# Scales by DMA, layer 1's weights split during layer 0, and layer 1's high part on ScalarE a unit late

## The chip, the cores and the metric

The kernel runs on one core of a Trainium2 chip. The metric is the device time in microseconds (us) of one execution, the median of several runs; less is better. The core's engines, each with its own queue of instructions that it works through in order, are TensorE (PE: matmuls; PEld: their weight loads), VectorE (DVE), ScalarE (ACT), GpSimd (POOL) and SyncE (SP, which here issues every DMA). TensorE has two clocks, 1.2 and 2.4 GHz; a "granted clock" of 1.00 is the higher one.

## The reference

All in float32. `x` is (2, 4096, 192), so 8192 tokens of 192 numbers.

```
conv:     out[s, h, :] = sum over k of softmax(weight[h])[k] * x[s - 6 + k, h, :]     (8 heads, 7 taps, causal)
layer 0:  h = conv @ w_in;   g = h * sigmoid(h);                        y = g @ w_out  (192 -> 2048 -> 192)
layer 1:  h = y @ w_in2;     g = h if h > 0 else exp(min(h, 0)) - 1;    out = g @ w_out2
```

The inputs arrive as float64 or float32 words laid out by the host; weights come as 64-bit words.

## The kernel before, in words

Tokens are cut into 16 blocks of 512 (`NB`), the 2048 inner columns into 8 pieces of 256 (`NQ`). A **unit** (layer, block, piece) is the work of one piece for one block: *in-products* (18 matmuls, `in_products`) make `h`, 256 x 512, in one of two PSUM buffers; `act_steps` makes `g` from it and splits `g` into a high part `g_hi`, in the type that TensorE multiplies, and a low part, the rest; *out-products* add the piece's share to four PSUM sums. Numbers are kept precise by such splits: a product is high x high plus high x low plus low x high. Layer 0 has 128 units, then layer 1 has 128. Blocks 0 and 1 of layer 0 go together in pairs at the start; block 2 uses full out-products of 20 matmuls. From block 3 of layer 0 on, and in all of layer 1, blocks are **scaled**: `g` is multiplied by a power of two `forth`, the low part is kept in float16 in a ring of 12 buffers, and a unit's out-products are only 12 matmuls (`high_products`); the low parts of a block's eight units are multiplied together at the end of the block (`low_products`, 32 + 64 short matmuls, lines 603 and 615). The sums are then scaled back, stored in memory after layer 0 and fetched again for layer 1.

The scale of a block needs the largest magnitudes over all 128 partitions: `measure` reduces on VectorE, GpSimd's `partition_all_reduce` (line 382) adds over the partitions, and `set_scale` makes `forth` and `back` with six tiny VectorE instructions (lines 411 to 419). The weights have such a scale too (`up`, `down`). Layer 0's output weights are brought to theirs by `rescale(q)` in units 19 to 26: ScalarE rounds them to float16 (line 215), VectorE makes the rest (lines 217, 221), ScalarE writes the rounded part back (line 225).

Order is written by hand. The main loop (line 1045) takes unit `s`: its in-products, the table `fill[s]` of side work, its `act_steps`, and the out-products of unit `s - LAG`, two units earlier. `at(step, f)` puts side work into the table; `where` is a unit's number. Side work is: the convolution taps on VectorE for the next block, splitting it (`split_conv`), fetching and splitting layer 1's input (`load_mid`, `split_mid`), and layer 1's weights. These are loaded once in blocks 5 to 8 to find their largest value (`measure_raw`), and again near the end of layer 0: from block 14 on `next_w` decodes piece q (64-bit words to float32: one ScalarE and three VectorE instructions, lines 138 to 149) and `split_w` splits it into `wi` and `wo` (ScalarE, GpSimd line 160, VectorE line 177), all inside the last units of layer 0 and the first of layer 1.

In layer 1 a unit's `act_steps` are, in this order:

```
ScalarE  g = relu(-h)            line 530        VectorE  g_hi = g * forth           line 535
ScalarE  g = exp(-g)             line 531        VectorE  lo = g * forth - g_hi      line 538
VectorE  g = max(g - 1, h)       line 532        (h's PSUM buffer is free after line 532)
```

In layer 0 they are silu in place (ScalarE, line 525), `g_hi` (ScalarE, line 526) and `lo` (VectorE, line 538, after which `h`'s buffer is free). As `h` has two buffers, the in-products of unit u + 2 wait until unit u has freed its own.

Of the kernel before, what the change touches and what calls it, by code (L numbers as in the profile page):

```python
# [40 lines left out]
RING = 12  # L41
# [5 lines left out]
def kernel(  # L47
# [114 lines left out]
    def split_w(layer, q, cols, eng, copy=None):  # L162
# [8 lines left out]
        if layer == 1:  # L171
            val = val[:, OUT].rearrange("p (i d) -> p i d", d=D)
            w16 = new_w16(layer, q)
            nc.scalar.activation(out=w16, in_=val, func=ACTF.Copy, scale=up[1])
            nc.scalar.activation(out=wo[:, :, 0:D], in_=w16, func=ACTF.Copy)
            for src, to in LOWS:
                nc.vector.scalar_tensor_tensor(
                    out=wo[:, :, to], in0=val[:, :, src], scalar=up[1], in1=wo[:, :, src].bitcast(F32),
                    op0=ALU.mult, op1=ALU.subtract,
                )  # L180
            return
# [9 lines left out]
    LOWS = (slice(P, D), slice(D, D + HP)), (slice(0, P), slice(D + HP, 2 * D))  # L191

# [18 lines left out]
    def rescale(q):  # L211
# [13 lines left out]
        nc.scalar.activation(out=wo[:, :, 0:D], in_=w16, func=ACTF.Copy)  # L225
# [182 lines left out]
    def set_scale(layer, b):  # L408
        t = stat[layer, b]
        total = small(tag="total")  # L410
        nc.vector.tensor_add(out=total, in0=t[:, 0:1], in1=t[:, 1:2])
# [9 lines left out]
    def set_weight_scale(layer, of):  # L421

        m = most[layer] = fixed.tile([P, 2], F32, tag=f"most{layer}", name="most")
# [6 lines left out]
        all_reduce(m, REDUCE.max)  # L430

    def finish_weight_scale(layer):
        largest = small(tag="total")
# [75 lines left out]

    def act_steps(u):  # L510

        h = h_t.pop(u)
        hi = gp.tile([P, 2, TB], F32R, tag="g_hi", name="g_hi")
        if scaled(*u[:2]):
# [4 lines left out]
        g = h if u[0] == 0 and u not in in_tmp else tmp.tile([P, 2, TB], F32, tag="g", name="g")  # L519
        g_of[u] = g  # L520
        if scaled(*u[:2]):
            s = forth[u[:2]]
            if u[0] == 0:
                steps = [
                    lambda: nc.scalar.activation(out=g, in_=h, func=ACTF.Silu),  # L525
                    lambda: nc.scalar.activation(out=hi, in_=g, func=ACTF.Copy, scale=s),  # L526
                ]
            else:
                steps = [
                    lambda: nc.scalar.activation(out=g, in_=h, func=ACTF.Relu, scale=-1.0),  # L530
                    lambda: nc.scalar.activation(out=g, in_=g, func=ACTF.Exp, scale=-1.0),  # L531
                    lambda: nc.vector.scalar_tensor_tensor(  # L532
                        out=g, in0=g, scalar=-1.0, in1=h, op0=ALU.add, op1=ALU.max
                    ),
                    lambda: nc.vector.tensor_scalar_mul(hi, g, s),  # L535
                ]
            return steps + [
                lambda: nc.vector.scalar_tensor_tensor(  # L538
                    out=lo, in0=g, scalar=s, in1=hi.bitcast(F32), op0=ALU.mult, op1=ALU.subtract
                )  # L540
            ]
        if u[0] == 0:
            steps = [
                lambda: nc.scalar.activation(out=hi, in_=h, func=ACTF.Silu),
                lambda: nc.scalar.activation(out=g, in_=h, func=ACTF.Silu),
            ]
        return steps + [lambda: nc.vector.tensor_sub(out=lo, in0=g, in1=hi.bitcast(F32))]
# [201 lines left out]
    LAG = 2  # L749
# [35 lines left out]
    for b in range(2, NB):  # L785
# [4 lines left out]
        if b >= NEW:  # L790
            steps += [lambda b=b: measure(0, b, conv_t[b, 0], conv_t[b, 1])]
            at(s - 1, lambda b=b: set_scale(0, b))
# [8 lines left out]
    at(TWO, lambda: set_weight_scale(0, found))  # L801
    at(TWO + LAG, lambda: finish_weight_scale(0))
    for q in range(NQ):
        at(TWO + LAG + 1 + q, lambda q=q: rescale(q))
        at(where[0, 5, 0] + 3 * q, lambda q=q: load_w(1, q))
        at(where[0, 5, 0] + 3 * q + 3, lambda q=q: measure_raw(q))
    at(where[0, 5, 0] + 3 * NQ, lambda: set_weight_scale(1, found))
    at(where[0, 5, 0] + 3 * NQ + 2, lambda: finish_weight_scale(1))

    def val_of_w2(q):
        if q in (3, 4):
            t = tmp.tile([P, 2, TB], F32, tag="g", name="val_g")
# [317 lines left out]
```

## Time and profile before

| | |
|---|---|
| median of 3 runs | 1134.26 us (1131.65 to 1134.41) |
| the profiled execution | 1132.55 us, of which the span is 1130.5 us, 2.05 us lie around it |
| TensorE matmul busy | 1087.0 us, 96% of the span |
| VectorE, ScalarE, GpSimd busy | 914.4 (81%), 679.6 (60%), 56.4 us (5%) |
| mean granted clock | 0.992 |
| DMA queue of SyncE | 66.06 MB, 21.7% of the 16 engines |

A busy share is a mean over stages with different limits; what a stage can win is read from the spacing of its matmuls. Every scaled block ends with the same low products, so the time from one block's to the next's is the time of a block.

### The profile page before, as it was taken

The numbers are of one execution on the slowest core, as the hardware profiler recorded it, in microseconds if no ns is written. First come the engines' busy times: TensorE is split into PE (matmuls) and PEld (weight loads), VectorE is DVE, ScalarE is ACT, GpSimd is POOL, SyncE is SP. The second block draws the span as 40 slices with busy tenths as digits, with TensorE's granted clock in tenths as the row PEclk, the third lists the DMA queues.
The fourth block names the chain that finished last, engine by engine and source line by source line (L and its number), as shares of the span: only waits on it lengthen the run. The fifth ranks groups of instructions, "written<-read, shape, count | busy, mean of one in ns | idle before, by whom it ended". The sixth has DMA issues, their size and how long they took to land.

```text
span 1130.5 us, 25043 instructions
## 1 busy us (share of the span) xinstructions
PE 1087.0 (96%) x10755; PEld 837.3 (74%) x10755; DVE 914.4 (81%) x1257; ACT 679.6 (60%) x773; POOL 56.4 (5%) x82
## 2 busy tenths in 40 slices
PE   7999889999999999989999999999999999999998
PEld 5998577777787777767767777777777776777776
DVE  6998676677777667668788988888988889888888
ACT  5764556655666666567875565555565565655654
POOL 4430000000000000000110000000000000000000
PEclk8999989999999999999999999999999999999999
DMA  4421023323322221254311111101111101111000
GB/s 126 149 51 49 23 56 86 82 88 100 99 57 57 57 57 30 54 143 124 102 35 33 38 52 53 52 18 50 38 52 52 50 18 39 52 52 52 25 25 15
DMA packets 41087, 67.65 MB, mean 60 GB/s; under 512 B 5392, under 2 KB 17936, under 8 KB 40976
## 3 DMA queue, kind: packets, MB, share of 16 engines
q1 hardware_dynamic: 40976, 66.06, 21.7%
q8 instruction: 84, 1.38, 0.5%
q14 instruction: 27, 0.22, 0.1%
HBM read 33.66 MB, written 12.58 MB: 41 GB/s over the span
## 4 chain that ended last, share of the span: by engine, by line
PE 57%; DVE 25%; issue 8%; ACT 7%; DMA 1%; SPq 1%; DVEq 0%; POOL 0%; ACTq 0%
PE h L503 27%; DVE g L532 10%; PE ab L591 9%; PE ab L615 9%; DVE g_hi L535 5%; PE c L603 5%; PE c L591 5%; DVE lo L538 3%; PE ab L664 2%; DVE x_hl L160 2%; ACT g L531 2%; DVE sum L387 2%; ACT g L530 2%; PE c L664 1%; DVE conv L458 1%
## 5 line engine op out<-in xcount | busy, mean ns | idle before, releaser
L503 PE MATMUL h<-x_hl,wi 64*128 64x512 f32 x4464 | 581.5, 392 | 32.9 <-DVE g L532 15.1
L503 PEld LDWEIGHTS h<-x_hl,wi 64*128 64x128 f32 x4464 | 433.0, 185 | 143.3 <-DVE g L532 28.8
L591 PE MATMUL ab<-g_hi,wo 64*128 64x512 f32 x1856 | 250.1, 387 | 0.0
L530 ACT ACTIVATE g<-h 128x1024 f32<-128x1024 f32 x128 | 131.6, 1028 | 163.1 <-PE h L503 160.5
L591 PEld LDWEIGHTS ab<-g_hi,wo 64*128 64x128 f32 x1856 | 175.8, 184 | 36.7 <-DVE mid_ab L710 0.4
L538 DVE SCALAR_TENSOR_TENSOR lo<-h,forth,g_hi 128x1024 f16<-128x1024 f32 x104 | 133.2, 1281 | 78.9 <-ACT g_hi L526 78.7
L532 DVE SCALAR_TENSOR_TENSOR g<-g,h 128x1024 f32<-128x1024 f32 x128 | 155.5, 1215 | 39.4 <-ACT g L531 36.4
L538 DVE SCALAR_TENSOR_TENSOR lo<-g,forth,g_hi 128x1024 f16<-128x1024 f32 x128 | 164.4, 1284 | 4.5
L525 ACT ACTIVATE h<-h 128x1024 f32<-128x1024 f32 x104 | 104.9, 1009 | 94.5 <-PE h L503 94.5
L591 PE MATMUL c<-g_hi,wo 64*128 64x512 f32 x928 | 144.4, 387 | 0.0
L531 ACT ACTIVATE g<-g 128x1024 f32<-128x1024 f32 x128 | 135.8, 1061 | 4.0
L526 ACT ACTIVATE g_hi<-h,forth 128x1024 fp32r<-128x1024 f32 x104 | 116.2, 1117 | 3.4
L458 DVE SCALAR_TENSOR_TENSOR conv<-x_raw,tap_w,conv 128x512 f32<-128x512 f32 (+1 forms) x174 | 103.8, 635 | 0.2
L591 PEld LDWEIGHTS c<-g_hi,wo 64*128 64x128 f32 x928 | 88.0, 185 | 18.5 <-issue 0.4
L615 PE MATMUL ab<-lo,w 64*64 64x512 f16 x1792 | 101.5, 376 | 0.0
L535 DVE TENSOR_SCALAR g_hi<-g,forth 128x1024 fp32r<-128x1024 f32 x128 | 97.0, 758 | 4.7
L615 PEld LDWEIGHTS <-w 64*64 64x64 f16 x1920 | 55.9, 107 | 44.4
L382 POOL PARTITION_ALL_REDUCE sum<-sum x29 | 11.9, 410 | 905.4 <-DVE sum L387 905.4
L603 PE MATMUL c<-lo,w 64*64 64x512 f16 x928 | 55.9, 379 | 0.0
L603 PEld LDWEIGHTS <-w 64*64 64x64 f16 x928 | 24.5, 106 | 27.7 <-issue 10.6
L715 ACT ACTIVATE o<-ab,back 128x512 f32<-128x512 f32 x16 | 11.0, 690 | 46.7 <-PE ab L615 41.5
L715 ACT ACTIVATE both<-c,back 128x512 f32<-128x512 f32 x29 | 19.9, 688 | 30.2 <-PE c L603 30.2
(135 smaller groups left out, 792.9 us busy)
## 6 DMA issues: line engine op xcount, KB each, us to landing
x_hl<-x_hl SPq DMA_DIRECT2D x60, 256.0 KB, 3.7
raw<-in_w_dram SPq DMA_DIRECT2D x21, 512.0 KB, 4.6
raw<-in_w_dram SPq DMA_DIRECT2D x51, 128.0 KB, 3.6
x_raw<-in_xT_dram SPq DMA_DIRECT2D x16, 259.0 KB, 4.0
kept_ab<-mid_ab SPq DMA_DIRECT2D x16, 256.0 KB, 2.0
mid_ab<-kept_ab SPq DMA_DIRECT2D x16, 256.0 KB, 4.0
mid_c<-kept_c SPq DMA_DIRECT2D x32, 128.0 KB, 3.8
x_hl<-x_hl SPq DMA_DIRECT2D x30, 128.0 KB, 3.8
```

What stands on the lines that cost most here:

```text
L458: nc.vector.scalar_tensor_tensor(out=y, in0=x, scalar=w, in1=y, op0=ALU.mult, op1=ALU.add)
L503: nc.tensor.matmul(out=h[:, r, :], lhsT=w[ROWS[r], w_lo, ts(of, P)], rhs=x_part(layer, b, 3 * x_lo + part)[ROWS[r], :], start=n == 0, stop ...
L525: lambda: nc.scalar.activation(out=g, in_=h, func=ACTF.Silu),
L526: lambda: nc.scalar.activation(out=hi, in_=g, func=ACTF.Copy, scale=s),
L530: lambda: nc.scalar.activation(out=g, in_=h, func=ACTF.Relu, scale=-1.0),
L531: lambda: nc.scalar.activation(out=g, in_=g, func=ACTF.Exp, scale=-1.0),
L532: lambda: nc.vector.scalar_tensor_tensor(out=g, in0=g, scalar=-1.0, in1=h, op0=ALU.add, op1=ALU.max),
L535: lambda: nc.vector.tensor_scalar_mul(hi, g, s),
L538: lambda: nc.vector.scalar_tensor_tensor(out=lo, in0=g, scalar=s, in1=hi.bitcast(F32), op0=ALU.mult, op1=ALU.subtract)
L591: nc.tensor.matmul(out=acc_t[layer, b, f"{name}{r}"], lhsT=wo[ROWS[r], i, ts(k, P)], rhs=hi[ROWS[r], i, :], start=q == 0 and n in (0, 2), ...
L603: nc.tensor.matmul(out=acc_t[layer, b, f"c{r}"][ROWS[i], :], lhsT=w16_t[layer, q][ROWS[r], i, P:D], rhs=g_t[u][1][ROWS[r], i, :], start=Fa ...
L615: nc.tensor.matmul(out=bank[ROWS[j], :], lhsT=w16_t[layer, q][ROWS[r], i, ts(j, HP)], rhs=g_t[u][1][ROWS[r], i, tokens], start=first and i ...
```

## The change

- **Scales.** `all_reduce` goes. `share` writes the 128 x 2 numbers to memory, `fetch` reads them back as 256 numbers on every partition, and a VectorE reduction over 256 columns takes the place of the first tiny instruction of `set_scale`. `fetch` is put two steps ahead of `set_scale`, `set_scale(1, b)` and `split_mid` one step earlier than before.
- **Layer 1's weights.** Piece by piece, one every five units from block 9 on, `made_steps` decodes and splits them in layer 0 (pieces 1 to 7, then 0) into one spare buffer and stores them in memory; in block 15 and the first units of layer 1 `bring` fetches them into the buffers that layer 0's pieces leave. Piece 0 stays where it was made. `rescale`'s last instruction becomes `rescale_end`, a unit later.
- **Layer 1's `act_steps`.** The high part becomes a ScalarE instruction, and it and the low part are held back until the next unit's `g` is made. `g` lies in the buffers of the raw weights.
- **Out-products** come three units late instead of two from unit 27 on (`turn` is 26, a step without any); one is made up for three units before the end. The ring has 11 buffers, `g_hi` uses six.

```
+    def made_steps(q):
...
+        return [
+            lambda: (mag(), low()),
+            lambda: (high(), last()),
+            lambda: copy(wi[:, 0, :], val[:, IN]),
+            lambda: lower(wi[:, 1, :], val[:, IN], wi[:, 0, :]),
+            lambda: nc.scalar.activation(out=w16, in_=v, func=ACTF.Copy, scale=up[1]),
+            lambda: copy(wo[:, :, 0:D], w16),
+            lambda: scale_low(*LOWS[0]),
+            lambda: scale_low(*LOWS[1]),
+            send,
+        ]
...
-    def all_reduce(t, op):
-        nc.gpsimd.partition_all_reduce(t, t, P, op)
+    def share(key, t):
+
+        shared[key] = tc.dram_tile([1, 2 * P], F32, name="shared")
+        nc.sync.dma_start(out=shared[key].rearrange("a (p n) -> (a p) n", n=2), in_=t)
+
+    def fetch(key):
+        t = fixed.tile([P, 2 * P], F32, tag="all", name="all")
+        nc.sync.dma_start(out=t, in_=shared[key].to_broadcast([P, 2 * P]))
+        shared[key] = t
...
-        nc.vector.tensor_add(out=total, in0=t[:, 0:1], in1=t[:, 1:2])
+        nc.vector.tensor_reduce(out=total, in_=shared[layer, b], axis=AX.X, op=ALU.add)
...
+        before = [held.pop(0) for _ in range(len(held))]
+        if u in units[-2:]:
+            before.append(lambda: nc.vector.tensor_scalar_mul(hi, g, s))
+            before.append(low)
+        else:
+            held.extend((high, low))
+        return steps + before
...
-        at(where[1, b, 0] - 5, lambda b=b: split_mid(b))
-        at(where[1, b, 0] - 1, lambda b=b: set_scale(1, b))
+        at(where[1, b, 0] - 6, lambda b=b: split_mid(b))
+        at(where[1, b, 0] - 4, lambda b=b: fetch((1, b)))
+        at(where[1, b, 0] - 2, lambda b=b: set_scale(1, b))
...
+        at(TWO + LAG + 2 + q, lambda q=q: rescale_end(q))
...
+    for k, q in enumerate([*range(1, NQ), 0]):
+        s = look + 8 + 5 * k
+        at(s - 7, lambda q=q: load_w(1, q))
+        at(s, lambda q=q: made.update({q: made_steps(q)}))
+        for i in range(9):
+            at(s + i // 2, lambda q=q, i=i: made[q][i]())
...
+        for k in range(2):
+            at(base + q + k * LATE, lambda q=q, k=k: bring(q, k))
```

How the order moves, at three places. **ScalarE in the middle of a block of layer 1**, two units before the change (L530 relu, L531 exp):

```order
L530 ACTIVATE g<-h 128x1024
L531 ACTIVATE g<-g 128x1024
L530 ACTIVATE g<-h 128x1024
L531 ACTIVATE g<-g 128x1024
L715 ACTIVATE both<-c_10428,back 128x512
```

and after it (L591 relu, L592 exp, L581 the high part):

```order
L591 ACTIVATE g<-h 128x1024
L592 ACTIVATE g<-g 128x1024
L581 ACTIVATE g_hi<-g,forth 128x1024
L591 ACTIVATE g<-h 128x1024
L592 ACTIVATE g<-g 128x1024
L581 ACTIVATE g_hi<-g,forth 128x1024
L771 ACTIVATE both<-c_11940,back 128x512
```

A third full-width instruction stands between two units; it belongs to the unit before.

**VectorE around the end of a block in layer 0**, from the sums (`both`, `mid_ab`) to the next unit's low part (`lo`), before:

```order
L706 SCALAR_TENSOR_TENSOR mid_ab<-ab_4511,back,mid_ab 128x512
L458 SCALAR_TENSOR_TENSOR conv<-x_raw,tap_w,conv 128x512
L458 SCALAR_TENSOR_TENSOR conv<-x_raw,tap_w,conv 128x256
L742 TENSOR_TENSOR other<-both,other 64x512
L458 SCALAR_TENSOR_TENSOR conv<-x_raw,tap_w,conv 128x512
L458 SCALAR_TENSOR_TENSOR conv<-x_raw,tap_w,conv 128x256
L458 SCALAR_TENSOR_TENSOR conv<-x_raw,tap_w,conv 128x512
L538 SCALAR_TENSOR_TENSOR lo_4942<-h,forth,g_hi 128x1024
```

and after, in block 10, where a piece of layer 1's weights is decoded (`val`) and split (`wi`) there:

```order
L762 SCALAR_TENSOR_TENSOR mid_ab<-ab_4599,back,mid_ab 128x512
L502 SCALAR_TENSOR_TENSOR conv<-x_raw,tap_w,conv 128x512
L502 SCALAR_TENSOR_TENSOR conv<-x_raw,tap_w,conv 128x256
L502 SCALAR_TENSOR_TENSOR conv<-x_raw,tap_w,conv 128x512
L140 TENSOR_SCALAR val<-raw 128x768
L144 TENSOR_SCALAR val<-raw 128x768
L148 SCALAR_TENSOR_TENSOR val<-mag,val 128x768
L798 TENSOR_TENSOR other<-both,other 64x512
L502 SCALAR_TENSOR_TENSOR conv<-x_raw,tap_w,conv 128x256
L428 TENSOR_REDUCE sum<-conv 128x1 x2
L367 TENSOR_TENSOR wi<-val,wi 128x384
L584 SCALAR_TENSOR_TENSOR lo_5070<-h,forth,g_hi 128x1024
```

Four instructions of the weights stand between the sums and `lo`, and the two reductions `sum` have moved ahead of this `lo`.

**ScalarE during the rescaling**, units 21 and 22 (`w_...` is the float16 part, `wo` the weights it goes back to, `g_hi` and `h` the two silus of block 2), before:

```order
L215 ACTIVATE w_1429<-wo,up 128x384
L225 ACTIVATE wo<-w_1429 128x2x192
L544 ACTIVATE g_hi<-h 128x1024
L545 ACTIVATE h<-h 128x1024
L215 ACTIVATE w_1480<-wo,up 128x384
L225 ACTIVATE wo<-w_1480 128x2x192
```

and after:

```order
L245 ACTIVATE w_1435<-wo,up 128x384
L574 ACTIVATE g_hi<-h 128x1024
L575 ACTIVATE h<-h 128x1024
L257 ACTIVATE wo<-w_1435 128x2x192
L245 ACTIVATE w_1488<-wo,up 128x384
```

The write back of `wo`, which needs VectorE's reading of the same weights, now stands behind the unit's two silus.

## Rows read from the trace of the kernel before

**Rows 1.** Windows: stretch; length; busy PE, PEld, DVE, ACT, POOL; PE clock; DMA share; GB/s.

```profile
400.00:450.00 50.00, 50.00 (x539) 37.47 (x536) 33.26 (x52) 30.16 (x34) 0.80 (x2) 1.00 0.19 49
700.00:750.00 50.00, 48.80 (x496) 36.59 (x496) 45.89 (x56) 28.62 (x31) 0.40 (x1) 1.00 0.11 30
```

**Rows 2.** Timeline (start, duration, instruction): first low products of blocks.

```profile
435.95 1.92 PE L603 MATMUL c<-lo,w 64*64 64x512 f16 x32
468.68 1.92 PE L603 MATMUL c<-lo,w 64*64 64x512 f16 x32
506.92 1.92 PE L603 MATMUL c<-lo,w 64*64 64x512 f16 x32
539.75 1.92 PE L603 MATMUL c<-lo,w 64*64 64x512 f16 x32
575.93 1.92 PE L603 MATMUL c<-lo,w 64*64 64x512 f16 x32
1091.79 1.92 PE L603 MATMUL c<-lo,w 64*64 64x512 f16 x32
```

**Rows 3.** Waits, 610 to 1120 us: waiter, releaser, total us, times, longest.

```profile
PE h L503 <- DVE g L532: 14.3, 24, 0.9
```

**Rows 4.** Groups by line and form: count, busy us, mean ns, idle before and releaser.

```profile
L535 DVE TENSOR_SCALAR g_hi<-g,forth 128x1024 fp32r<-128x1024 f32 x128 | 97.0, 758 | 4.7
L526 ACT ACTIVATE g_hi<-h,forth 128x1024 fp32r<-128x1024 f32 x104 | 116.2, 1117 | 3.4
L530 ACT ACTIVATE g<-h 128x1024 f32<-128x1024 f32 x128 | 131.6, 1028 | 163.1 <-PE h L503 160.5 <-DVE g L532 2.6
L531 ACT ACTIVATE g<-g 128x1024 f32<-128x1024 f32 x128 | 135.8, 1061 | 4.0
L532 DVE SCALAR_TENSOR_TENSOR g<-g,h 128x1024 f32<-128x1024 f32 x128 | 155.5, 1215 | 39.4 <-ACT g L531 36.4 <-issue 2.7
```

**Rows 5.** Timeline of layer 0: in-products of two units, a low part between.

```profile
444.78 2.20 PE L503 MATMUL h<-x_hl,wi 64*128 64x512 f32 x18
446.14 1.27 DVE L538 SCALAR_TENSOR_TENSOR lo<-h,forth,g_hi 128x1024 f16<-128x1024 f32 x1
448.18 2.20 PE L503 MATMUL h<-x_hl,wi 64*128 64x512 f32 x18
```

**Rows 6.** Timeline: late weights in layer 0, on ScalarE.

```profile
493.89 0.91 ACT L138 ACTIVATE mag<-raw 128x768 f32<-128x768 f32 x1 [5.18 <-DMA raw<-in_w_dram]
```

**Rows 7.** Timeline: decoding and splitting one piece of layer 1's weights.

```profile
547.16 0.59 DVE L141 TENSOR_SCALAR val_x<-raw 128x768 uint16<-128x768 uint16 x1
548.35 0.96 DVE L149 SCALAR_TENSOR_TENSOR val_x<-mag,val_x 128x768 int32<-128x768 int32 x1
553.16 0.74 DVE L177 SCALAR_TENSOR_TENSOR wo<-val,up,wo 128x128 fp32r<-128x128 f32 x2
```

**Rows 8.** Timeline: in-products of units 20 and 28, around the rescaling.

```profile
105.18 0.39 PE L503 MATMUL h<-x_hl,wi 64*128 64x512 f32 x1
151.17 3.99 PE L503 MATMUL h<-x_hl,wi 64*128 64x512 f32 x18 [5.23 <-DVE lo L538]
```

**Rows 9.** Waits of the whole span, as in rows 3.

```profile
ACT wo L225 <- DVE more L217: 19.5, 8, 3.5
```

**Rows 10.** DMA issues: tensors, queue, count, KB each, median us to landing.

```profile
raw<-in_w_dram SPq DMA_DIRECT2D x21, 512.0 KB, 4.6
kept_c<-other SPq DMA_DIRECT2D x16, 128.0 KB, 2.3
tap_raw<-in_taps_dram SPq DMA_DIRECT2D x1, 7.0 KB, 1.6
```

**Rows 11.** Groups by line and form, as in rows 4: a small reduction.

```profile
L387 DVE TENSOR_REDUCE sum<-conv 128x1 f32<-128x256 f32 x13 | 5.3, 404 | 0.0
```

**Rows 12.** Timeline: end of the measuring and first tiny instruction of one scale.

```profile
447.73 1.00 DVE L387 TENSOR_REDUCE sum<-conv 128x1 f32<-128x512 f32 x2
460.62 0.15 DVE L411 TENSOR_TENSOR total<-sum 128x1 f32<-128x1 f32 x1
```

More of the change, by code (lines that the diff above doesn't have):

```diff
@@ L40 @@
 NEW = 3
-RING = 12
+RING = 11
 EXP = 0x7F800000
@@ L389, in measure @@
             )
-        all_reduce(t, REDUCE.add)
+        share((layer, b), t)
     def power(out, of, exponent):
@@ L421, in set_weight_scale @@
     def set_weight_scale(layer, of):
-        m = most[layer] = fixed.tile([P, 2], F32, tag=f"most{layer}", name="most")
+        m = fixed.tile([P, 2], F32, tag=f"own{layer}", name="own")
         nc.vector.tensor_reduce(out=m, in_=of, axis=AX.X, op=ALU.max)
@@ L429, in set_weight_scale @@
             )
-        all_reduce(m, REDUCE.max)
+        share(layer, m)
     def finish_weight_scale(layer):
+        m = most[layer] = fixed.tile([P, 2], F32, tag=f"most{layer}", name="most")
+        nc.vector.tensor_reduce(
+            out=m, in_=shared[layer].rearrange("p (n two) -> p two n", two=2), axis=AX.X, op=ALU.max
+        )
         largest = small(tag="total")
@@ L508, in in_products @@
         return [[lambda r=r, n=n: product(r, n) for n in range(len(order))] for r in range(2)]
+    held = []
     def act_steps(u):
         h = h_t.pop(u)
-        hi = gp.tile([P, 2, TB], F32R, tag="g_hi", name="g_hi")
-        if scaled(*u[:2]):
+        new = scaled(*u[:2])
+        hi = gp.tile([P, 2, TB], F32R, tag=f"g_{'lo' if new and where[u] % 2 else 'hi'}", name="g_hi")
+        if new:
             lo = ring.tile([P, 2, TB], F16, tag=f"lo{where[u] % RING}", name="lo16")
@@ L542, in act_steps @@
-        if u[0] == 0:
-            steps = [
+        if new and u[0] == 1:
+            g = raw.tile([P, W_IN + W_OUT], I64, tag="raw", name="g").bitcast(F32)[:, 0 : 2 * TB]
+            g = g.rearrange("p (i t) -> p i t", i=2)
+        else:
+            g = h if u not in in_tmp else tmp.tile([P, 2, TB], F32, tag="g", name="g")
+        g_of[u] = g
+        if not new:
+            return [
                 lambda: nc.scalar.activation(out=hi, in_=h, func=ACTF.Silu),
                 lambda: nc.scalar.activation(out=g, in_=h, func=ACTF.Silu),
+                lambda: nc.vector.tensor_sub(out=lo, in0=g, in1=hi.bitcast(F32)),
@@ L546, in act_steps, with high, low @@
             ]
-        return steps + [lambda: nc.vector.tensor_sub(out=lo, in0=g, in1=hi.bitcast(F32))]
+        s = forth[u[:2]]
+        def high():
+            nc.scalar.activation(out=hi, in_=g, func=ACTF.Copy, scale=s)
+        def low():
+            nc.vector.scalar_tensor_tensor(
+                out=lo, in0=g, scalar=s, in1=hi.bitcast(F32), op0=ALU.mult, op1=ALU.subtract
+            )
+        if u[0] == 0:
+            return [lambda: nc.scalar.activation(out=g, in_=h, func=ACTF.Silu), high, low]
@@ L1043 @@
         products(out_products(units[TWO + 1]))
+        turn = where[0, NEW, 0] + LAG
         for s in range(TWO + 4, n_units):
-            u, done = units[s], units[s - LAG]
+            u = units[s]
             if s < n_units - 2:
@@ L1049 @@
             if s in (n_units - 3, n_units - 2):
+                if s == n_units - 3:
+                    products(high_products(units[s - LATE]))
                 products(in_products(units[s + 1]))
             act = act_steps(u)
+            if s == turn:
+                run(fill.get(s, ()))
+                run(act)
+                continue
+            done = units[s - (LATE if turn < s < n_units - 3 else LAG)]
             new = scaled(*done[:2])
```

107 lines of the change are left out of this document (48 added, 59 removed).

## The prediction, made before the changed kernel was run

> **What bounds the kernel now.** The windows come first: in the middle of layer 0 TensorE's records fill 50.00 of 50 us and VectorE is busy 33.26; in layer 1 VectorE is busy 45.89 and TensorE's records leave gaps [rows 1]. Next the timeline of one line: the first low products come once a block, so their spacing is the time of a block. In quiet layer 0 it is 468.68 - 435.95 = 32.73 us; over fifteen blocks, from 575.93 to 1091.79, it is 515.86, 34.39 each [rows 2]. A block has the same matmuls in both layers, so 32.73 is what TensorE needs and 34.39 - 32.73 = 1.66 us per block is waiting. The waits name its source: in layer 1 TensorE stops 24 times before in-products, 14.3 us in all, for the instruction that makes `g` on VectorE, L532 [rows 3]; the rest of the 24.9 us (15 x 1.66) I put down to the restarts, since a weight load that waits is no longer hidden. So layer 0 is bound by TensorE, layer 1 by VectorE's queue. Three places in layer 0 have gaps of their own: the block from 468.68 to 506.92 took 38.24 (5.51 too long), the one from 539.75 to 575.93 took 36.18 (3.45 too long) [rows 2], and the stretch of the rescaling, below.
>
> **Layer 1, the high part.** VectorE loses L535, 128 x 758 ns = 97.0 us, so 8 x 0.758 = 6.06 us of its block; the 0.40 us reduction over 256 columns, once a block, gives back 0.4 at most [rows 4, 11]. From 45.89 busy in 50 us, 31.5 of a 34.39 us block, VectorE falls to about 25.9 of 32.73: no longer the bound. ScalarE gains eight copies. No row shows one from SBUF to SBUF with a scale read from memory; the row of layer 0, which reads PSUM, has 1.117 [rows 4]. Relu reads PSUM in 1.028 and exp SBUF in 1.061, so SBUF may add 0.03: between 1.06 and 1.15, and I take 1.12. Per unit ScalarE then has 1.028 + 1.061 + 1.12 = 3.21 us. TensorE's unit is 448.18 - 444.78 = 3.40 [rows 5], so ScalarE keeps up by 0.19 a unit. It also has five half-width instructions a block, at most 5 x 0.75 us (an estimate, above half of 1.117); they stand where the low products give it 32.73 - 8 x 3.40 = 5.5 us more. In all at most 29.4 of 32.73. What the change moves is behind the path: relu, exp, L532 still free `h` after 1.03 + 1.06 + 1.22 = 3.31 us, and in-products of u + 2 come 3.40 + 3.40 - 2.1 = 4.7 us after those of u end (2.1, 18 of a unit's 30 matmuls, is how long they hold TensorE). What stood in front of L532 was L535 and the low part of the unit before; now only the low part does. The out-products read the high part a unit later, which is what three late is for. I take the floor of layer 0: 15 x 1.66 = **-24.9**. Bounds: -26.5 (the sixteenth block too) and -12 (half is left).
>
> **Weights in layer 0 instead of at its end.** ScalarE's decode at 493.89 had waited 5.18 us for its load [rows 6]; the load now goes out seven units ahead, 24 us, against 4.6 to land [rows 10]. That block's 5.51 goes, and the 3.45 of the block in which four engines split weights goes too: **-9.0** (bounds -5, -9.5). In their place come fetches of 0.39 MB, two a unit, needed eight units later; they cost nothing unless SyncE holds back something more urgent.
>
> The work moves into blocks 9 to 13, where TensorE had no gap. One piece costs VectorE 2.15 us for decoding (547.16 to 549.31), less than 0.96 for the 384-column subtraction, 0.74 for the two low parts [rows 7], so about 3.5 us; eight are 28 us, beside 33.26 busy of 50. On average it fits: 66% and 28 / 164 = 17%. In order it doesn't always. VectorE's low part (1.27) frees `h` in layer 0; at 447.41 it is done, 448.18 the matmuls start [rows 5], so 0.77 us are to spare, and a unit leaves VectorE 3.40 - 1.27 = 2.1 us for side work, of which taps take 1 to 2. The eight pieces begin five units apart, so each begins at another of the eight steps of a block. The step without taps hides its decode. Two of them (the end of a block and the unit behind it, where sums and taps already delay VectorE) lose nearly all of 2.15, some 2 us each; the step with `set_scale` 1.2; the other four 0.2 to 0.6 each. With restarts I take **+8**. Bounds: +1 (all hidden) and +24 (eight times 3: nothing hidden).
>
> **The rescaling.** ScalarE waited 19.5 us in eight stops for VectorE before it wrote `wo` back, each ahead of a unit's silus [rows 9]. From the in-products of unit 20 to those of unit 28, 105.18 to 151.17, 45.99 us pass [rows 8]. A matmul takes 3.40 / 30 = 0.113 us; six units of 38 matmuls (full out-products) and two of 30 need 6 x 4.3 + 2 x 3.4 = 32.6, so 13.4 are lost. With the write back behind the silus the chain of ScalarE and VectorE falls apart in units 20 to 25. What stays is VectorE's queue in steps 25 and 26: the two sums' end, five taps and two rescales still stand ahead of unit 26's low part, for which unit 28 waits; I keep 4 of the 13.4. The out-products left out at `turn` (12 x 0.113 = 1.36) come back at the end of the kernel. So -13.4 + 4 + 1.36 = **-8** (bounds -11, -2; behind the last stop 18 matmuls took 3.99 us against 2.20 [rows 5, 8], which I leave as it is).
>
> **Scales by DMA.** GpSimd's sum came early enough: the first tiny instruction ran 11.9 us after the measuring (460.62 - 448.73) [rows 12]. The new way is a write, a wait of SyncE for it, a read: 2.3 us for a store, up to 4.6 for a load [rows 10], 7 with the issues. It has the time between the measuring and the first tiny instruction: these 11.9 us in layer 0, and four units, 13.6, in layer 1. Hidden, except in blocks 5 to 12: there raw weights (three DMAs, 4.6) go out just ahead of `fetch` in SyncE's queue, and 7 + 4.6 is 11.6 of 11.9. While VectorE waits, the taps and the unit's low part are queued behind it, and TensorE behind that. I take **+1.5** (0 to +6). The pieces of 8 bytes are not in any row; the smallest transfer, 56 bytes per partition, landed in 1.6 us [rows 10], so I price them as any store. The Trainium skill speaks against that: "DMA: Bandwidth & Descriptors", Specifications, has transfers under 512 bytes done by reading, changing and writing back. No run here shows it; it is weighed as a rival below.
>
> **Sum.** Against the profiled execution, 1132.55: -24.9 - 9.0 + 8 - 8 + 1.5 = -32.4, so 1100.2. The median of the runs lay 1.7 above that execution; **1102 us**.
>
> **Rivals.**
> - *Layer 0 can't hold the weights* (0.15). VectorE's delays carry over from unit to unit, and with ScalarE's four pieces of each weight they cost the bound, +24 instead of +8: 1118. For it: no slack is above 0.77 us. Against: the step without taps and the low products let VectorE catch up.
> - *ScalarE takes VectorE's place in layer 1* (0.12). With 3.21 of 3.40 us a late start is made good by 0.19 a unit only; if half of the 1.66 stays, 12.5 more: 1114. For it: relu waits for TensorE, then the copy of the unit before stands behind exp. Against: 5.5 us of low products a block.
> - *Nothing collides* (0.07): +1 and 0 instead of +8 and +1.5, rescaling at its bound: 1102 - 7 - 1.5 - 3 = 1090.
> - *The scales come late* (0.04), the slower one. `set_scale` stands in VectorE's in-order queue, 29 times. If the round trip exceeds its cover of 11.9 to 13.6 us, the excess falls on every block: to lose the whole gain of 32 us, 1.1 us each time, so a round trip of about 14 us instead of 7, twice what the rows give. At 16 us, 29 x 2.8 = 81 less the 32: 1151 if all of it passes through. That is where this rule of the Trainium skill would lead.
> - *No effect* (0.03): gains in layer 1 eaten by both of the first two: about 1132.
>
> **How the numbers follow.** The forecast has 0.59. Its own range is 1095 to 1110. From 1091 to 1118 the forecast's cases, the first two rivals and part of the third are held, eight in ten. This kernel's measurement can't tell less than 0.3%, 3.4 us, from no change. Faster 0.93 (forecast and first three), same 0.03, slower 0.04.
>
> **What would show it.** Right: blocks of layer 1 at 32.7 to 33 us, with no stop for `g`; no gap where rows 6 stand; VectorE near 40 of 50 us in layer 1. The weights: stops of TensorE for `lo` in blocks 9 to 13, two of about 2 us. The scales: VectorE's 256-column reduction not waiting for a DMA; if it does in every block, the last rival holds. Wrong: blocks of layer 1 above 33.5 with ScalarE's relu starting late; or a sum of stops in blocks 9 to 13 above 15 us.

## The result, and the profile after

The changed kernel took 1120.2 us (median of 4 runs, 1118.67 to 1121.2), the kernel before 1134.16 beside it: ratio 0.9881, 95% interval 0.9862 to 0.9899. It is faster by 14 us (1.2%) where 32 were forecast, and 1120.2 lies above the forecast's range of 1095 to 1110. The profiled execution's span is 1118.8 us, 11.7 below that of before.

Windows first, as in [rows 1] (stretch; length; busy PE, PEld, DVE, ACT, POOL; PE clock; DMA share; GB/s):

```profile
400.00:450.00 50.00, 44.70 (x410) 33.57 (x408) 35.53 (x62) 29.99 (x36) 0.00 (x0) 0.93 0.48 125
700.00:750.00 50.00, 50.00 (x492) 39.43 (x490) 38.10 (x45) 44.00 (x45) 0.00 (x0) 1.00 0.19 46
```

The two layers have changed places. In layer 1 TensorE's records now fill all 50 us; VectorE fell from 45.89 to 38.10, ScalarE rose to 44.00. In layer 0 TensorE has 5.3 us of gaps where it had none, at a granted clock of 0.93. The first low products, as in [rows 2], say how much in which block:

```profile
336.13 1.92 PE L659 MATMUL c<-lo,w 64*64 64x512 f16 x32
377.94 1.92 PE L659 MATMUL c<-lo,w 64*64 64x512 f16 x32
415.73 1.92 PE L659 MATMUL c<-lo,w 64*64 64x512 f16 x32
456.43 1.92 PE L659 MATMUL c<-lo,w 64*64 64x512 f16 x32
558.09 1.92 PE L659 MATMUL c<-lo,w 64*64 64x512 f16 x32
591.63 1.92 PE L659 MATMUL c<-lo,w 64*64 64x512 f16 x32
1082.53 1.92 PE L659 MATMUL c<-lo,w 64*64 64x512 f16 x32
```

Fifteen blocks of layer 1 take 1082.53 - 591.63 = 490.90, 32.73 each. I call this the floor, as it is also the time of a block in the quiet part of layer 0 before [rows 2]. Blocks 9, 10 and 11 of layer 0 take 41.81, 37.79 and 40.70. The next table has every kernel that was run. Its last three columns are us lost in these blocks: the spacing of the same products, less 32.73 a block (blocks 14 and 15 are the last of layer 0, block 16 is the first of layer 1). "Start" is the time of the first such product, at the end of block 3. These columns come from one profile of each kernel.

| kernel | us, median | ratio to before, 95% | start | blocks 5-8 | 9-13 | 14-16 |
|---|---|---|---|---|---|---|
| before | 1134.16 | 1 | 173.5 | 0.6 | 5.5 | 5.2 |
| after | 1120.2 | 0.9862-0.9899 | 164.0 | 8.5 | 25.6 | 0.8 |
| e1 early store | 1110.13 | 0.9768-0.9826 | 165.4 | 7.1 | 12.7 | 1.5 |
| e3 GpSimd scales | 1102.16 | 0.9698-0.9744 | 166.5 | 1.5 | 11.9 | 0.3 |
| e4 weights as before | 1106.92 | 0.9737-0.9793 | 163.9 | 6.7 | 9.9 | 5.5 |
| e5 e1 + later split | 1112.78 | 0.9785-0.9834 | 163.9 | 7.3 | 17.6 | 2.0 |
| e6 e1 + e3 | 1100.37 | 0.9691-0.9734 | 167.0 | 1.5 | 10.0 | 0.3 |
| e7 e5 + e3 | 1099.31 | 0.9669-0.9709 | 166.8 | 1.5 | 9.2 | 0.3 |
| e8 rescaling alone | 1121.03 | 0.9874-0.9922 | 160.7 | 0.6 | 6.4 | 5.1 |
| e9 e3 + e4 | 1100.53 | 0.9686-0.9734 | 167.1 | 1.0 | 5.4 | 5.0 |
| e10 scales, GpSimd's queue | 1111.8 | 0.9793-0.9854 | 164.1 | 2.1 | 19.7 | 1.9 |
| e11 e6, six apart | 1102.74 | 0.9699-0.9740 | 167.0 | 2.0 | 8.9 | 4.0 |
| e12 e7, six apart | 1098.0 | 0.9655-0.9704 | 166.2 | 1.5 | 6.5 | 2.1 |
| e13 e12, later turn | 1098.23 | 0.9646-0.9698 | 163.6 | 1.5 | 6.6 | 2.0 |
| e14 e1 + e10 | 1103.24 | 0.9718-0.9750 | 163.7 | 5.3 | 11.8 | 1.4 |
| e15 e12, scales as e10 | 1099.05 | 0.9690-0.9718 | 161.4 | 3.8 | 7.3 | 4.0 |

(In e13 block 4 loses 2.8 besides; elsewhere it loses nothing.)

Where did after's 25.6 and 8.5 come from? The waits of its whole span (waiter, releaser, total us, times, longest):

```profile
ACT wi L364 <- DMA kept_wi<-wi: 18.6, 4, 7.6
ACT wi L364 <- DVE val L148: 8.3, 5, 3.2
...
PE h L547 <- DVE lo L584: 25.4, 18, 5.6
...
DVE total L451 <- DMA all<-shared: 7.3, 4, 2.1
```

TensorE's stops are for `lo` on VectorE, as forecast, but in blocks 9 to 13 eight of them sum to 16.4 us, above the 15 that I had named as the sign of being wrong. And two things that stand ahead of `lo` are not VectorE's work: ScalarE waits for a *store* of weights to land, and VectorE for the scales. This is the longest of the first kind, in block 9, from all engines' timelines (L192 makes the last part of the piece, L203 stores it):

```profile
346.58 0.73 DVE L192 SCALAR_TENSOR_TENSOR wo<-val,up,wo 128x128 fp32r<-128x128 f32 x2
349.17 3.02 SPq L315 DMA_DIRECT2D x_hl<-x_hl  x4
352.24 0.63 SPq L203 DMA_DIRECT2D kept_wi<-wi  x1
356.62 1.70 SPq L101 DMA_DIRECT2D raw<-in_w_dram  x2
360.74 0.52 ACT L364 ACTIVATE wi<-val 128x384 fp32r<-128x384 f32 x1 [7.64 <-DMA kept_wi<-wi]
361.30 0.56 DVE L367 TENSOR_TENSOR wi<-val,wi 128x384 fp32r<-128x384 f32 x1 [5.50 <-ACT wi L364]
364.70 4.21 PE L547 MATMUL h<-x_hl,wi 64*128 64x512 f32 x18 [5.63 <-DVE lo L584]
```

All pieces are made in one spare buffer. Piece k is stored at the end of its last step, and ScalarE's copy of piece k + 1 into the same buffer comes two units, 6.8 us, later. Here the piece was done at 347.31, but its store went out 4.9 us later: SyncE works through its issues in order, and raw words and the exchange (`x_hl`, copies between partitions) stood ahead. The store then took 8.4 us to land; until then ScalarE stands, the silu of the next unit behind it, VectorE behind that, TensorE last. The other three stores that were waited for stood 3.2, 4.3 and 11.3 us in SyncE's queue (the last behind a wait for a block's sums) and landed in 7.5, 4.7 and 3.8. The 18 matmuls after the stop take 4.21 us instead of 2.20 [rows 5]: the clock has fallen to its lower level (granted 0.50 from 364.70 to 368.90), and over the whole block it is 0.92. In the table of windows that is 36.14 us of TensorE for work that took 33.27 a block earlier:

```profile
302.00:336.10 34.10, 33.27 (x338) 24.99 (x336) 25.87 (x45) 21.37 (x25) 0.00 (x0) 1.00 0.37 98
336.10:377.90 41.80, 36.14 (x338) 27.50 (x336) 26.38 (x44) 23.23 (x29) 0.00 (x0) 0.92 0.42 117
```

A stop of 5.63 us costs some 2.9 more in that way. The second kind, in block 5, on SyncE, VectorE and TensorE (L418 stores the scale's sums, L422 loads them):

```profile
206.27 1.00 DVE L428 TENSOR_REDUCE sum<-conv 128x1 f32<-128x512 f32 x2
207.29 0.33 SPq L418 DMA_DIRECT2D shared<-sum  x1
207.67 1.29 SPq L101 DMA_DIRECT2D raw<-in_w_dram  x2
209.00 0.59 SPq L107 DMA_DIRECT2D raw<-in_w_dram  x1
209.98 3.75 SPq L315 DMA_DIRECT2D x_hl<-x_hl  x4
213.78 0.59 SPq L422 DMA_DIRECT2D all<-shared  x1
221.82 0.42 DVE L451 TENSOR_REDUCE total<-all 128x1 f32<-128x256 f32 x1 [2.13 <-DMA all<-shared]
225.55 2.34 PE L547 MATMUL h<-x_hl,wi 64*128 64x512 f32 x18 [1.07 <-DVE lo L584]
```

From the measuring's end at 207.27 to the reduction at 221.82 pass 14.6 us; I had 11.6 against a cover of 11.9. The load goes out 6.5 us after the store, not because SyncE waits for the store (in blocks 5 to 13 that came to 2.3 us in two places) but because seven other issues stand between, four of them the exchange, at 0.9 us each; then 8 us pass until it has landed, among raw weights. DMA issues, as in [rows 10]:

```profile
all<-shared SPq DMA_DIRECT2D x31, 128.0 KB, 4.3
...
kept_wi<-wi SPq DMA_DIRECT2D x7, 384.0 KB, 6.0
kept_wo<-wo SPq DMA_DIRECT2D x7, 384.0 KB, 6.4
...
shared<-sum SPq DMA_DIRECT2D x29, 1.0 KB, 5.1
```

The 1 KB of a scale, in pieces of 8 bytes, takes 5.1 us to land, where a store of 128 KB took 2.3 before [rows 10]. That is the direction of the rule of the Trainium skill, "DMA: Bandwidth & Descriptors", Specifications, that transfers under 512 bytes are read, changed and written back: the trace agrees in the direction, 5.1 us against 2.3, but no run shows that this is the reason.

### The profile page after: what moved, and what is told of

It reads as the page before. It is cut to its first block, busy times and chain, and to the rows that moved or that the text cites. A ratio compares the mean times of both kernels' runs of the same rounds, so it can differ in the third digit from the quotient of the medians.

```text
span 1118.8 us, 25134 instructions
## 1 busy us (share of the span) xinstructions
PE 1084.3 (97%) x10755; PEld 838.9 (75%) x10755; DVE 823.4 (74%) x1141; ACT 809.8 (72%) x899; POOL 34.4 (3%) x43
## 4 chain that ended last, share of the span: by engine, by line
PE 76%; DVE 10%; DMA 6%; ACT 3%; issue 2%; SPq 2%; DVEq 0%; ACTq 0%
PE h L547 37%; PE ab L647 14%; PE ab L671 9%; PE c L647 7%; PE c L659 5%; DVE lo L584 3%; DVE conv L502 2%; DMA all<-shared 2%; DMA kept_wi<-wi 2%; PE ab L720 2%; PE c L720 1%; DMA x_hl<-x_hl 1%; DMA shared<-sum 1%; PE ab L628 1%; ACT g_hi L581 1%
## 5 line engine op out<-in xcount | busy, mean ns | idle before, releaser
L547 PEld LDWEIGHTS h<-x_hl,wi 64*128 64x128 f32 x4464 | 440.7, 186 | 129.4 <-DVE lo L584 34.9
L647 PE MATMUL ab<-g_hi,wo 64*128 64x512 f32 x1856 | 249.5, 388 | 0.0
L584 DVE SCALAR_TENSOR_TENSOR lo<-g,forth,g_hi 128x1024 f16<-128x1024 f32 x128 | 163.6, 1278 | 0.1
L591 ACT ACTIVATE g<-h 128x1024 f32<-128x1024 f32 x128 | 131.7, 1029 | 42.9 <-PE h L547 42.9
L581 ACT ACTIVATE g_hi<-g,forth 128x1024 fp32r<-128x1024 f32 x126 | 143.1, 1136 | 0.0
L592 ACT ACTIVATE g<-g 128x1024 f32<-128x1024 f32 x128 | 135.7, 1060 | 4.0
L581 ACT ACTIVATE g_hi<-h,forth 128x1024 fp32r<-128x1024 f32 x104 | 116.1, 1116 | 3.4
L574 ACT ACTIVATE g_hi<-h 128x1024 fp32r<-128x1024 f32 x22 | 22.5, 1024 | 27.9 <-PE h L547 27.9
L720 PE MATMUL ab<-g_hi,wo 64*128 64x512 f32 x128 | 35.4, 395 | 0.0
```

Of the source, the lines that this page charges most:

```text
L547: nc.tensor.matmul(out=h[:, r, :], lhsT=w[ROWS[r], w_lo, ts(of, P)], rhs=x_part(layer, b, 3 * x_lo + part)[ROWS[r], :], start=n == 0, stop ...
L584: nc.vector.scalar_tensor_tensor(out=lo, in0=g, scalar=s, in1=hi.bitcast(F32), op0=ALU.mult, op1=ALU.subtract)
L647: nc.tensor.matmul(out=acc_t[layer, b, f"{name}{r}"], lhsT=wo[ROWS[r], i, ts(k, P)], rhs=hi[ROWS[r], i, :], start=q == 0 and n in (0, 2), ...
L720: ins = nc.tensor.matmul(out=acc_t[0, b, name][0 : cols.stop - cols.start, :], lhsT=wo[ROWS[r], i, cols], rhs=g_t[0, b, q][part][ROWS[r], ...
```

## The experiments

**Theory:** the made weights lose time by the store that holds the one buffer, and the scales by where their transfers stand in SyncE's queue. **Rivals:** ScalarE and VectorE simply have too much to do in blocks 9 to 13; the raw weights, not the scales, are late in blocks 5 to 8.

**e1, early store.** `wi` goes out as soon as it is split, three units earlier, `wo` a unit earlier.

```
-            lambda: lower(wi[:, 1, :], val[:, IN], wi[:, 0, :]),
+            lambda: (lower(wi[:, 1, :], val[:, IN], wi[:, 0, :]), send("wi", wi)),
...
-            lambda: scale_low(*LOWS[1]),
-            send,
+            lambda: (scale_low(*LOWS[1]), send("wo", wo)),
```

> Changed kernel, but each made piece's in-projection half is stored as soon as it is split (a step after its decode) and its out-projection half a step earlier than now, instead of both at the end of the piece. Theory (the next piece's copy into the single spare place waits for the last store, 18.6 us of ScalarE waits in four places): those four waits fall below 3 us in all, the two long TensorE stops of 5.6 and 3.1 us go, blocks 9 to 13 take about 12 us less than their 189.2, and the kernel about 1108 us. Rival (ScalarE and VectorE have simply too much to do in these blocks, the store's place is a symptom): blocks 9 to 13 give back under 4 us, the kernel stays at 1116 or above.

1110.13 us; blocks 9 to 13 lost 12.7 instead of 25.6, about the expected 12 less; no wait for a store of weights is left among ScalarE's. So the stores' place is a cause and the rival falls as the whole account, though ScalarE's waits for VectorE's decode (`val`) rose there from 5.6 to 10.5 us. The stores also landed sooner (DMA issues of blocks 9 to 13):

```profile
kept_wi<-wi SPq DMA_DIRECT2D x7, 384.0 KB, 3.3
kept_wo<-wo SPq DMA_DIRECT2D x7, 384.0 KB, 3.0
```

**e3, scales by GpSimd**, the rest as changed.

```
...
-        nc.sync.dma_start(out=shared[key].rearrange("a (p n) -> (a p) n", n=2), in_=t)
+        nc.gpsimd.partition_all_reduce(t, t, P, op)
...
```

> Changed kernel, with the maxima and sums over partitions taken by GpSimd as before, so that no 1 KB store and load lies between a measurement and its scale. Theory (the round trip through memory is late: VectorE waited 7.3 us in four places for it, blocks 5 to 8 are 8.5 us over their floor): blocks 5 to 8 come within 2 us of the floor of 4 x 32.73, the kernel takes about 1113 us. Rival (the loads and reductions of layer 1's raw weights, which stand in blocks 5 to 7, are what is late there, as they were not in the kernel before only because other things were later): blocks 5 to 8 stay 6 us or more above the floor, 1119 or above. Blocks 9 to 13 move by under 4 us either way, or the traffic of the scales had a part there too.

1102.16 us, 18 less than after where 7 were expected. Blocks 5 to 8 came to 1.5, as the theory had it, with the raw weights still in them: that rival falls. But blocks 9 to 13 fell by 13.7 as well: the scales' traffic had a part in the first loss too. ScalarE's waits for stores fell from 18.6 to 8.7 us.

**e4, weights as before**, the rest as changed (`split_w` in place of `made_steps`, a unit later than before since out-products are later).

> Changed kernel, with layer 1's weights decoded and split around the change of layers as in the kernel before (nothing made in blocks 9 to 13, no store of weights, no fetch); the rest stays as changed. Theory (making the weights in blocks 9 to 13 costs about 25 us where I had put 8): blocks 9 to 13 fall to 33 to 34 us each, the stops at the change of layers come back with about 9 us, and the kernel takes about 1104 us. Rival (what the five blocks lost comes from the scales' transfers and from the order of ScalarE's work, not from the weights): they stay above 36 us each, and with the 9 us that come back the kernel takes 1122 us or more.

1106.92 us. Blocks 9 to 12 at the floor; the change of layers lost 15.4 (9.9 in block 13, 5.5 behind it) instead of the 9 I had put back. So without the made weights blocks 9 to 12 lose nothing, though the scales' transfers are still there, and the version that moves the weights is slower by 13 us than the one that doesn't.

**e5, early store and later split**: the copy of `wi` two units after the decode.

```
-            at(s + i // 2, lambda q=q, i=i: made[q][i]())
+            at(s + (i + 2 * (i > 1)) // 2, lambda q=q, i=i: made[q][i]())
```

> As the run with the early stores, and besides the split of a piece starts two steps after its decode instead of one, so that ScalarE comes to the copy when VectorE's decode is long done. Theory (what the early store leaves is ScalarE standing in order behind VectorE's decode, 8.3 us in five places, with the activation that TensorE needs queued behind it): blocks 9 to 13 take about 20 us less than their 189.2, the kernel about 1100 us. Rival (VectorE has no time left there: with the copy moved, its lower parts come late just the same): no more than 3 us below the run with the early stores alone.

1112.78 us: a miss. In blocks 9 to 13 the waits for `val` were down to 1.2 us, but block 9 took 40.7 again, for the other reason (VectorE and TensorE of e5):

```profile
361.43 0.42 DVE L449 TENSOR_REDUCE total<-all 128x1 f32<-128x256 f32 x1 [5.09 <-DMA all<-shared]
...
365.63 4.21 PE L545 MATMUL h<-x_hl,wi 64*128 64x512 f32 x18 [3.15 <-DVE lo L582]
```

VectorE now stood 5.09 us for the scale, whose load was late.

**e6, e1 and e3 together.**

> Both repairs together: the made pieces are stored early and the scales are taken by GpSimd. Theory (two causes that add in part: with the scales off the queue, 8.7 us of ScalarE waits for the stores were left in blocks 9 to 13, and the early store took away such waits): blocks 9 to 13 fall from 11.9 us over their floor to 4 to 7, and the kernel takes about 1096 us. Rival (both repairs removed the same delay, stores held up in the queue): the kernel stays at 1101 us or above.

1100.37 us, 10.0 lost in blocks 9 to 13. Between the two, nearer the rival: each repair alone took 13 to 14 off, both 15.6. They remove mostly one delay, and the traces of e1 and e6 show where it comes from. In both the store goes out early, with the raw words right behind it; in e1 the scale's store stands just ahead (SyncE of e1, then of e6):

```profile
346.76 0.33 SPq L416 DMA_DIRECT2D shared<-sum  x1
347.45 0.33 SPq L202 DMA_DIRECT2D kept_wo<-wo  x1
...
343.42 0.33 SPq L203 DMA_DIRECT2D kept_wo<-wo  x1
343.80 1.29 SPq L102 DMA_DIRECT2D raw<-in_w_dram  x2
```

In e1 this store took 5.5 us to land, in e6 2.3. In layer 1, where neither raw words nor made weights move, the stores of the results go out right behind the scale's, and the same is seen (DMA issues from 640 to 1060 us, of after, then of e3):

```profile
out_dram<-o SPq DMA_DIRECT2D x13, 256.0 KB, 6.1
out_dram<-other SPq DMA_DIRECT2D x13, 128.0 KB, 5.6
shared<-sum SPq DMA_DIRECT2D x13, 1.0 KB, 5.6
...
out_dram<-o SPq DMA_DIRECT2D x13, 256.0 KB, 2.7
out_dram<-other SPq DMA_DIRECT2D x13, 128.0 KB, 2.5
```

So the 1 KB store makes large stores beside it late by some 3 us. Where nobody waits for them, as in layer 1, that costs nothing. What stays of the 10.0 stands, for example, here (ScalarE and TensorE of e6):

```profile
375.97 0.53 ACT L363 ACTIVATE wi<-val 128x384 fp32r<-128x384 f32 x1 [3.16 <-DVE val L149]
...
379.92 3.59 PE L541 MATMUL h<-x_hl,wi 64*128 64x512 f32 x18 [2.27 <-DVE lo L578]
```

Behind a block's end VectorE comes late to the decode, and ScalarE's copy waits for it ahead of the unit's silu. This is the collision that I had forecast.

**e8, the rescaling alone**: before, with the copy back of `wo` a step later.

> The kernel before with one edit alone: ScalarE's copy back of a rescaled out-projection is issued a step after the scaling, in place of directly behind it. Theory (the copy waits in order for three VectorE operations and holds the next activation): the units 20 to 28 take about 10 us less than their 45.99, some 1 us comes back, and the kernel takes 1124 to 1126 us. Rival (the 10 us that these units lost less in the changed kernel came from the scales' other path, as GpSimd no longer stands between): under 3 us, 1131 or above.

1121.03 us, 12.6 less than before where 8 to 10 were expected (by the interval 8.8 to 14.3); the rival falls. Units 20 to 28 take 35.64 us as in the changed kernel; another 1.7 comes from the 18 matmuls behind their last stop, 2.33 us instead of 3.99 [rows 8]. The one stop left is 2.58 us, and the clock holds behind it:

```profile
140.03 2.33 PE L505 MATMUL h<-x_hl,wi 64*128 64x512 f32 x18 [2.58 <-DVE lo L540]
```

**e9, scales and weights as before**; what is left is the high part on ScalarE with later out-products, and the rescaling.

> Changed kernel with layer 1's weights made as before and the scales taken by GpSimd as before: what is left of the change is the high part on ScalarE, the later out-products and the later copy back. Theory (the scales' transfers cost 6 to 7 us in blocks 5 to 8, and GpSimd's scales begin layer 0 some 2.5 us later): about 1103 us, against 1107 with the scales by transfer. Rival (the 18 us that GpSimd's scales gave were all due to the made weights): 1106 or above. If it is below 1100, blocks 9 to 13 or the change of layers took part too.

1100.53 us, 2.5 below the theory and 6.4 below e4: most of it in blocks 5 to 8 (6.7 to 1.0) and at the change of layers (15.4 to 10.5). Against e6 (1100.37) it is the same: with everything repaired, making the weights in layer 0 gains nothing, as it loses 10.0 + 0.3 in blocks 9 to 16 and the old way loses 5.4 + 5.0.

**e10, the scales' transfers issued by GpSimd.**

```
...
-        nc.sync.dma_start(out=t, in_=shared[key].to_broadcast([P, 2 * P]))
+        nc.gpsimd.dma_start(out=t, in_=shared[key].to_broadcast([P, 2 * P]))
...
```

> Changed kernel, with the store and the load of the scales issued by GpSimd, which is idle, in place of SyncE; the transfers themselves stay. Theory (SyncE waits in order for the 1 KB store to land before it may issue the load, and holds the raw loads, the exchanges and the stores of made weights behind it): most of what GpSimd's own sums gave comes back, the kernel takes 1104 to 1108 us and the waits for the stores of made weights fall below 10 us. Rival (it is the round trip's own length, 5 and 4 us, that is late): VectorE waits for the sums as before, blocks 5 to 8 stay 6 us or more above their floor, and the kernel takes 1115 or above.

1111.8 us, between the two. In blocks 5 to 8 the loss was 2.1, though a store and a load still took 3.5 and 4.5 us, and VectorE waited for no sum there: it was the queue. In blocks 9 to 13 19.7 stayed, with 13.1 us of ScalarE's waits for late stores: the three that were waited for took 4.2 to 7.3 us to land, against 3.3 to 5.5 in e3, so the scale's transfers delay them from another queue as well.

**e14, e10 with early stores**, to tell whether that rest is the transfers' or the stores'.

> Changed kernel, with the early stores and with the scales' transfers issued by idle GpSimd. Theory (the scales cost what they hold up in SyncE's queue, and the rest is the wait for late stores): blocks 9 to 13 as with early stores and GpSimd's own sums (173.6 us, within 2), and, as layer 0's scaled blocks begin some 2.5 us earlier than with GpSimd's sums, the kernel 1097 to 1101 us. Rival (the transfers themselves, 1 KB in pieces of 8 bytes and 128 KB back, slow the other transfers): blocks 9 to 13 stay 6 us or more above 173.6, the kernel 1104 or above.

1103.24 us, between the two. Blocks 9 to 13 at 11.8, within 2 of e6: the rest was the wait for late stores. The rival is right that the transfers slow others (see e6), but that costs little once nothing waits for the stores. But blocks 5 to 8, the same code as in e10, lost 5.3, and there VectorE waited 3.2 us in two places for sums that came on an idle queue, one load taking 8.3 us. Over all profiles these blocks lost 6.7 to 8.5 with the scales on SyncE's queue (4 profiles), 2.1 to 5.3 on GpSimd's (3), 1.0 to 2.0 with GpSimd's sums (7). The queue is the larger part in two of the three; the transfers' own time has a part, and one profile of each doesn't size it.

**e7, e11, e12: late split and wider spacing with GpSimd's scales** (`s = look + 8 + 6 * k` in e11 and e12).

> Early stores, the scales on GpSimd, and the split of a made piece two steps after its decode. Theory (what the run with both repairs has left over its floor in blocks 9 to 13, 9.9 us with all of it behind four TensorE stops, is ScalarE standing behind VectorE's decode for 10.2 us; in the run with the late split it was the load of a scale, 5.09 us of VectorE in block 9, that hid the gain): blocks 9 to 13 within 4 us of the floor in all, the kernel 1093 to 1096 us. Rival (VectorE has no room for the pieces, so the stop only moves): 1099 or above.

> Early stores and GpSimd's scales, with the pieces six units apart instead of five (block 14 takes part of the work). Theory (each stop comes where a split meets the end of a block, whatever the spacing): eight pieces meet the block ends as often, 1098 to 1101 us. Rival (the stops come from the density of the work): the same pieces spread over one block more cost 4 us less, 1096 or below.

> All of it: early stores, GpSimd's scales, the split two steps after the decode, pieces six units apart. Theory: as the run with pieces five apart and the late split, within 2 us. Rival (density): 2 us or more below it.

1099.31, 1102.74 and 1098.0 us. e7: in blocks 9 to 13 ScalarE's waits for `val` fell from 10.2 to 1.2, TensorE's stops from 5.6 to 5.5 only: the stop moves, as the rival had it. e11 is 2.4 above e6, beside both expectations. e12 is 1.3 below e7, as its theory had it.

**e13, `turn` a block later; e15, e12 with the scales as in e10.**

> The version with everything repaired, and the step from which out-products run three units late, which has no out-products of its own, moved one block further, from block 3's to block 4's third unit. Theory (the TensorE stop of 3.98 us there and the slower products after it, 3.78 for 2.3, come from VectorE's rescaling of layer 0's weights, which stands in the same units; a block later VectorE is free): the stop is under 1 us, the kernel takes 1093 to 1095 us. Rival (two in-products in a row need a product buffer that only VectorE's lower part sets free, whatever else it does): the stop moves along, 1097 to 1099.

> The repaired version with pieces six units apart and the split two steps after the decode, but the scales by transfer on GpSimd's queue in place of GpSimd's sums. Theory (an idle queue hides the round trip): 1094 to 1098 us, 0 to 3 us below the same version with GpSimd's sums (1098.0). Rival (the transfers are late in blocks 9 to 14, where VectorE would stand for the sums): 1101 or above.

1098.23 and 1099.05 us: no gain. In e13 the stop in the rescaling shrank only from 3.98 to 2.61, and the step without out-products cost 2.8 in block 4 instead. The 1.37 of difference is the time of the 12 matmuls that are left out there in e12 (1.36): what VectorE sets is when unit 28 may start, and TensorE only came to it earlier. e15 is between its two cases; its earlier start is given back in blocks 5 to 16. e12, e13 and e15 can't be told apart; e12, at 0.9679 of before and 22 us below after, beats both kernels. It is not shown to beat e9, whose interval overlaps with its own.

## Why the prediction was wrong

By its terms, against the spans (1130.5 and 1118.8; negative is time won):

| step | predicted | measured |
|---|---|---|
| layer 1, high part on ScalarE | -24.9 | -25.0 (515.9 to 490.9, fifteen blocks) |
| late weights gone | -9.0 | -8.2 (5.51, and 3.45 to 0.81) |
| weights made in blocks 9 to 13 | +8 | +25.6 |
| rescaling | -8 | -9.0 (units 20 to 28: 45.99 to 35.64, and 1.36 back) |
| scales by DMA | +1.5 | +5.4 (+7.8 in blocks 5 to 8, -2.4 ahead of unit 20) |
| rest | 0 | -0.5 (-0.4 of it in the last block) |
| sum | -32.4 | -11.7 |

("Start" moved by 9.5 only, less than the last rows add up to: as out-products are later now, TensorE has made 18 in-products more by then, 630 against 612. These 2.0 us come back at the kernel's end.)

- *Layer 1* was right in size and mechanism. ScalarE's copy from SBUF took 1136 ns where I took 1.12:

```profile
L581 ACT ACTIVATE g_hi<-g,forth 128x1024 fp32r<-128x1024 f32 x126 | 143.1, 1136 | 0.0
```

  The waits show no stop of TensorE between 600 and 1110 us. VectorE is at 38.1 of 50, near the 40 named as the sign. The rival that ScalarE takes its place falls.
- *Rescaling* was right in mechanism and nearly in size: from unit 20 to 28 it is 35.64 us against 45.99 [rows 8], and 35.64 in e8, which has this edit alone.

```profile
102.74 2.39 PE L547 MATMUL h<-x_hl,wi 64*128 64x512 f32 x18
...
138.38 3.91 PE L547 MATMUL h<-x_hl,wi 64*128 64x512 f32 x18 [3.98 <-DVE lo L584]
```

  That the stop is 3.98 where I kept 4 is partly luck: 2.6 of it are VectorE's (e8, e13), the rest is what `turn` leaves out. I counted the 1.36 that `turn` gives back, but not that it saves them here first.
- *The step that failed: weights in layer 0.* "One piece costs VectorE 2.15 us for decoding ..." counted the collisions in VectorE's queue, and these came: with the store early and the scales on GpSimd, 10.0 are lost. What it left out is `send`. I priced the fetches and the decode but not the 0.39 MB stores as something that is *waited for*: the copy of the next piece writes the buffer that the store reads. Two units, 6.8 us, lie between; but the stores that were waited for stood 3.2 to 11.3 us in SyncE's queue and then took 3.8 to 8.4 to land, where the one row I had is 2.3 for a third of the bytes. e1 showed it: 12.9 of the 25.6. The rival "layer 0 can't hold the weights" had the right sign and, with +24, nearly the size, for another reason.
- *The step that also failed: scales by DMA.* "7 + 4.6 is 11.6 of 11.9" left out SyncE's own time: the load goes out 6.5 us after the store, with seven issues between, and needs 8 to land beside the raw words. With 14.6 against the cover the sum came 2.13 late. The +7.8 of these blocks lies above the bound of +6. The term was also taken by itself, while e3 gave 18 us, of which 13.7 lie in blocks 9 to 13: there the scale's store makes the stores of weights late. Round trips of 14 us are what the slower rival named, but VectorE waited for only 4 of 29 sums, three of them in blocks 5 to 8. (Its own price was wrong: 81 on top of 1102 is 1183; 1151 takes off the 32 a second time.)
- *A gain that I had not seen* is the -2.4 ahead of unit 20: without GpSimd's sums GpSimd begins earlier. Its first long instruction makes `diag`, for which TensorE waits 4.4 us in the kernel before (GpSimd of before, then of after):

```profile
8.34 1.91 POOL L859 TENSOR_SCALAR_AFFINE_SELECT diag<-tap_w 128x896 f32<-128x896 f32 x2 [7.35 <-ACT tap L472]
...
4.06 1.91 POOL L909 TENSOR_SCALAR_AFFINE_SELECT diag<-tap_w 128x896 f32<-128x896 f32 x2 [3.06 <-DVE tap_w L278]
```

  It starts at 8.3 to 8.6 us in all nine kernels with `partition_all_reduce` and at 3.9 to 4.1 in all seven without; no run shows why. This is why "start" is mostly later with GpSimd's sums. With it the whole term, +5.4, falls within its bounds, by luck.

The two terms that held sum to -32.9, and e9, which is these two alone, measured -33.1. The net that I gave for weights and scales was +0.5, and it was +19.7 (1120.2 - 1100.53).

Open: why a store of 1 KB in pieces of 8 bytes delays the large stores beside it, and why GpSimd begins later in kernels with `partition_all_reduce`. That the rest in blocks 9 to 13 is collisions in VectorE's queue is read from traces; no run took them away, and the made weights' cost in blocks 9 to 16 could not be brought below 8.6 us (e12).

## What to carry to other kernels

A store is not free because nobody reads it soon: whoever writes its buffer next waits for it to land, so send it at once and count the units until the next writer. Count also the issues that stand ahead of it in its queue. Price a round trip through memory with the issues that stand between its two halves, and with the transfers it runs beside, not with a row from a quiet stretch; and ask what a small transfer does to the large ones beside it. Of the change's parts two made all the gain; measure each alone before keeping the rest.

## What the runs showed of the hardware

- A store of 384 KB landed in 5.5 us where the 1 KB store of a scale, in 8-byte pieces, went out just ahead of it (e1), and in 2.3 us at the same place without (e6). In layer 1 stores of 256 and 128 KB took 6.1 and 5.6 us behind such a store (after), 6.1 and 5.8 when another queue issued it (e10), and 2.7 and 2.5 without (e3). The 1 KB store itself took 3.5 (e10, blocks 5 to 8) to 5.6 us (after, layer 1).
- GpSimd's first long instruction started at 8.3 to 8.6 us in nine kernels with `partition_all_reduce`, at 3.9 to 4.1 us in seven without.
- After stops of 3.98 and 5.63 us, 18 matmuls took 3.91 and 4.21 us, against 2.20 at the full clock; after 2.58 us they took 2.33 (e8), after 2.27 once 3.59 (e6).
